# Fourier mixing beside attention on one core: the hidden-dimension transform by sums and differences of features n and n + 224

## The chip, the cores and the metric

The kernel runs on one core of a Trainium2 chip. The metric is the device time of one execution in microseconds (us); the time of a kernel is the median over its runs. Engines: TensorE (PE; PEld is its weight load), VectorE (DVE), ScalarE (ACT), GpSimd (POOL) and SyncE (SP), whose queue issues every DMA of this kernel.

## The reference

Two independent halves, written side by side. A is a two-dimensional Fourier transform of `x` (2048 tokens by 448 features), real part only, by given matrices; B is attention with 16 heads of 28 features over 2048 tokens.

```python
# S = 2048, D = 448; everything float32
a = einsum("bsd,ed->bse", A_x, dft_hid_re)
b = einsum("bsd,ed->bse", A_x, dft_hid_im)
A = einsum("ts,bse->bte", dft_seq_re, a) - einsum("ts,bse->bte", dft_seq_im, b)
q, k, v = (B_x @ wqkv) split into 3 x 16 heads of 28
B = concat_heads(softmax(q @ k.T * 28 ** -0.5) @ v) @ wo
out = concatenate([A, B], axis=-1)
```

## The kernel before

**Products in parts.** TensorE multiplies in a reduced float format. To keep float32 accuracy an operand is split: `hi` is its rounded copy (made by ScalarE) and `lo` the rest (made by VectorE), and a product is hi x hi + lo x hi + hi x lo. With 448 features in the contraction (three blocks of 128 rows and one of 64, whose hi and lo share a block) that makes 11 products where three full ones would be 12.

**Stages.** In TensorE's order: the projections of `B_x` (L572, `chain`), then A's hidden transform (`hidden_both`, also through `chain`, L572), then the sequence transform of A in two parts, real and imaginary (`sequence_halved`, L909), each with a small middle row (`middle`, L857), and the output projection of B (`project_late`, L1372, and its last feature block, L1403). All of these are "fill work" around the attention: scores (`score`, L1138: one 128 x 512 product each, 1024 of them), exponentials on ScalarE (L1142), and attention times values (`four`, L1149). The latter runs in 64 bursts of 16 products, one burst per 16 exponentials. A burst of a whole chunk is followed by a normalization (`normal`): ScalarE copies the sums out (L1202), and DMAs carry them through memory (`sm`, L1206; `rd`, L1211; spread over partitions, L1215), VectorE multiplies (L1218), and the result goes to memory (L1221). The last head is handled chunk by chunk: its four chunks are folded by TensorE first (L1229), and `project_late` loads the last 64 features of each chunk (L1390), splits them (L1392, L1393) and adds their products (L1403, 8 per chunk, two per token tile).

**The hidden transform.** For each of 16 token tiles the features of the tile arrive with one DMA (`Piece`, L542) in a `wraw` buffer. The wanted 896 columns (448 real, 448 imaginary) are symmetric: column 448 - n equals column n up to sign. So only `MAIN` = 225 columns of each half (450) are computed in full with 11 products; for the other `REST` = 223 (446) four products with a difference table `w_rest` (all but zero for true Fourier matrices) are computed. That is 15 products per tile. The tables are built by `weights_both`, which also records the largest magnitude of the difference tables in `diff`. At the end of the kernel a flag is computed from `diff`; if the matrices are not what the symmetry assumes, a slower general path runs after it. With the given inputs it does not.

**Combining.** `combine` loads the stored results of tiles g and g + 8 (L788), copies two of them (L792), and forms sums and differences (L794, L795) which it splits (L797 hi on ScalarE, L798 lo on VectorE) into operands of the sequence transform, in the large buffer `big`. There are 8 groups g for each of the two parts, and with 4 copies a group 32 copies a part on ScalarE. The sequence transform's own weights come in units of four DMAs (L891), of which three go to buffers (`wdraw`) that lie where the hidden tables were, so they wait for the last hidden product.

**Buffers.** `kept` has 19 buffers of 128 x 1024 floats; each holds two exponential tiles, or a stored result, or a load. There are eight PSUM banks: four for fill work and four for scores, which may borrow from the former.

**What sets the order.** A planner in the kernel (`Schedule`) emits all instructions of all engines in one list, before the program runs. Every task has a key (a due time), durations and latencies; at each modelled moment an engine takes the ready task with the lowest key for which buffers are free. Constants set the keys: `T_ATT` and `T_END` spread the heads' scores, `T_FILL` the fill work, `T_OUT` the end, and `PE_TURN` and the 0.2146 per product are modelled prices of a burst. A DMA task without `hold` may be issued as soon as SP is idle and a buffer is free. On the chip each engine runs its list in order and waits on semaphores.

Of the kernel before, what the change touches and what calls it, by code (L numbers as in the profile page):

```python
# [14 lines left out]
ALU = mybir.AluOpType  # L15
# [48 lines left out]
def f32(ap):  # L64
    return ap.bitcast(F32)
# [16 lines left out]
PE_TURN = 0.33  # L82
# [231 lines left out]
def tile_kernel(ctx, tc, xa, wre, wim, wd, xb, wqkv, wo, out):  # L314
# [75 lines left out]
    nc.gpsimd.memset(diff[:, 2 * NQ, 4:3 * QT], 0.0)  # L390
# [51 lines left out]
    T_ATT, T_END, T_FILL, T_OUT = 28.0, 723.0, 850.0, 801.0  # L442
# [19 lines left out]
    F_HIDDEN = NT * 15 * M448  # L462
# [259 lines left out]
    w_hi = wd_t[:, :8 * MAIN].rearrange("p (k c) -> p k c", k=4)  # L722
    w_rest = wd_t[:, 8 * MAIN:8 * D].rearrange("p (k c) -> p k c", k=4)
    w_lo = big[:, 7 * S:7 * S + 8 * MAIN].rearrange("p (k c) -> p k c", k=4)

    def weights_both(key, after):
        ready = []
        for k in range(4):
            pair = kept_s.slot()
            at = key + 0.6 * k  # L730
            n = P if k < 3 else 64
            main = lambda t, n=P: t[:n].rearrange("p (a b) -> p a b", a=2)
            ld = dma(at, lambda pair=pair, k=k: nc.sync.dma_start(pair.t[:, :, :D], wd[:, k].rearrange("p (a b) -> p a b", a=2)), 448, use=[pair])
            a = act(at, lambda pair=pair, k=k: nc.scalar.activation(main(w_hi[:, k]), pair.t[:, :, :MAIN], AF.Copy), 0.45,
                    deps=[ld, *after], use=[pair])
            ts = [dve(at, lambda pair=pair, k=k, n=n: nc.vector.tensor_tensor(
                main(w_lo[:, k], n), pair.t[:n, :, :MAIN], main(f32(w_hi)[:, k], n), op=ALU.subtract), 0.55, deps=[a], use=[pair])]
            for i, op in ((0, ALU.subtract), (1, ALU.add)):
                ts.append(dve(at, lambda pair=pair, k=k, i=i, op=op: nc.vector.tensor_tensor(
                    w_rest[:, k, i * REST:(i + 1) * REST], pair.t[:, i, MAIN:D], back(pair.t[:, i], 1, REST), op=op), 0.3,  # L740
                    deps=[ld, *after], use=[pair]))
            seen.append(dve(at + 5, lambda k=k: nc.vector.tensor_reduce(
                diff[:, 2 * NQ, k:k + 1], f32(w_rest)[:, k], axis=AX.X, op=ALU.max, apply_absolute_value=True), 0.55, deps=ts))
            if k == 0:
                seen.append(dve(at + 5, lambda: nc.vector.tensor_reduce(
                    whole[:, 2 * NQ:2 * NQ + 1], f32(w_hi)[:, 0], axis=AX.X, op=ALU.max, apply_absolute_value=True), 0.55, deps=[a]))
# [747 lines left out]
```

## Time and profile before

| | |
|---|---|
| time, median of 3 runs | 825.43 us (825.27 to 826.31) |
| the profiled execution's own time | 829.04 us |
| its span, first to last instruction | 827.2 us |
| mean granted TensorE clock | 0.991 |
| TensorE matmul instructions in the trace | 4856 |

An instruction of the kernel's text on TensorE can appear as more than one row: attention times values has 1024 products in the program and 2048 rows in the trace. In a row of the groups by line the columns are line, engine, operation, tiles, shapes and count, then busy time and mean duration of one in ns, then idle time of the engine before them and what ended it. In a row of a window they are the stretch, its length, and for PE, PEld, DVE, ACT and POOL the busy time and count, then granted clock, DMA share and GB/s. In the chain of waits a row is a start, a length and what ran; in the timeline also the shape. TensorE's durations overlap (matmuls are pipelined), so what one costs is read from the distance between starts.

### The profile page before, as it was taken

The numbers are of one execution on the slowest core, as the hardware profiler recorded it, in microseconds if no ns is written. First come the engines' busy times: TensorE is split into PE (matmuls) and PEld (weight loads), VectorE is DVE, ScalarE is ACT, GpSimd is POOL, SyncE is SP. The second block draws the span as 40 slices with busy tenths as digits, with TensorE's granted clock in tenths as the row PEclk, the third lists the DMA queues.
The fourth block names the chain that finished last, engine by engine and source line by source line (L and its number), as shares of the span: only waits on it lengthen the run. The fifth ranks groups of instructions, "written<-read, shape, count | busy, mean of one in ns | idle before, by whom it ended". The sixth has DMA issues, their size and how long they took to land.

```text
span 827.2 us, 14140 instructions
## 1 busy us (share of the span) xinstructions
PE 814.4 (98%) x4856; PEld 531.0 (64%) x4856; DVE 383.2 (46%) x882; ACT 622.9 (75%) x1277; POOL 8.3 (1%) x59
## 2 busy tenths in 40 slices
PE   8999999999999999999989999999999999999996
PEld 7886555655566666656655675666766656665686
DVE  7541103123112134222367774566887585575561
ACT  6116888889888777878888877778997777778931
POOL 3000000000000000000000000000000000000000
PEclk9999999999999999999988999999999999999998
DMA  9847635334344434433487755359877756652643
GB/s 307 280 139 239 192 107 169 97 105 141 103 150 122 131 123 135 136 134 122 143 195 228 244 160 175 117 169 275 210 227 232 213 165 200 198 188 83 198 152 128
DMA packets 131535, 141.27 MB, mean 171 GB/s; under 512 B 36414, under 2 KB 100416, under 8 KB 131456
## 3 DMA queue, kind: packets, MB, share of 16 engines
q1 hardware_dynamic: 131456, 140.29, 54.7%
q8 instruction: 40, 0.66, 0.3%
q14 instruction: 39, 0.32, 0.1%
HBM read 98.82 MB, written 43.12 MB: 172 GB/s over the span
## 4 chain that ended last, share of the span: by engine, by line
PE 88%; ACT 5%; DMA 4%; DVE 1%; issue 1%; SPq 0%; ACTq 0%; DVEq 0%
PE bank L1138 28%; PE bank L1149 25%; PE bank L572 19%; PE bank L909 9%; PE bank L1372 4%; ACT kept L1142 3%; DMA wdraw<-wre 2%; PE bank L857 1%; PE bank L1122 1%; DMA wraw<-wre 1%; ACT big L797 1%; PE bank L1403 1%; DMA kept<-xb 1%; ACT big L792 1%; PE bank L1229 0%
## 5 line engine op out<-in xcount | busy, mean ns | idle before, releaser
L1142 ACT ACTIVATE kept<-bank 128x512 f32<-128x512 f32 x1024 | 511.1, 677 | 118.8 <-PE bank L1138 118.4
L1138 PE MATMUL bank<-q,k 85*128 85x512 f32 x1024 | 371.0, 409 | 1.6 <-DVE kept L1125 0.9
L1138 PEld LDWEIGHTS bank<-q,k 85*128 85x128 f32 x1024 | 186.4, 189 | 98.3 <-issue 42.0
L1149 PE MATMUL bank<-kept,v 128*32 128x512 f32 x2048 | 237.6, 605 | 0.0
L1149 PEld LDWEIGHTS bank<-kept,v 128*32 128x32 f32 x2048 | 60.8, 111 | 134.9 <-issue 127.6
L909 PE MATMUL bank<-big,wlo 128*128 128x226 f32 x512 | 104.4, 277 | 1.0 <-DVE wlo L899 1.0
L909 PEld LDWEIGHTS bank<-big,wlo 128*128 128x128 f32 x512 | 95.7, 198 | 9.8 <-DVE wlo L899 1.3
L572 PE MATMUL bank<-big,whi 128*128 128x512 f32 (+1 forms) x260 | 96.6, 392 | 0.9 <-ACT big L511 0.7
L909 PE MATMUL bank<-big,whi 128*128 128x448 f32 (+1 forms) x256 | 74.8, 325 | 1.1 <-DVE big L798 1.1
L881 DVE TENSOR_REDUCE diff<-wlo 128x1 f32<-128x512 f32 x96 | 65.5, 683 | 2.5
L439 DVE COPY kept<-bank 128x450 f32<-128x450 f32 (+2 forms) x43 | 26.7, 620 | 81.7 <-PE bank L572 71.1
L572 PEld LDWEIGHTS bank<-big,whi 128*128 128x128 f32 x260 | 49.3, 191 | 9.7 <-ACT big L511 1.1
L909 PEld LDWEIGHTS bank<-big,whi 128*128 128x128 f32 x256 | 49.1, 198 | 6.3 <-DVE big L798 1.4
L572 PE MATMUL bank<-big,wlo 128*128 128x512 f32 x112 | 44.2, 396 | 0.0
L614 DVE TENSOR_TENSOR wd<-bank,wd 128x512 fp32r<-128x512 f32 x16 | 10.9, 690 | 69.8 <-ACT wd L613 69.8
L572 PE MATMUL bank<-wd,whi 128*128 128x450 f32 (+1 forms) x128 | 41.6, 368 | 0.0
L899 DVE TENSOR_TENSOR wlo<-wraw,whi 128x512 fp32r<-128x512 f32 x32 | 22.1, 690 | 38.5 <-PE bank L909 34.8
L572 PE MATMUL bank<-wd,big 128*128 128x448 f32 x176 | 37.6, 370 | 0.0
L572 PEld LDWEIGHTS bank<-wd,big 128*128 128x128 f32 x176 | 32.9, 188 | 3.9 <-issue 0.7
L1372 PE MATMUL bank<-big 128*128 128x448 f32 x144 | 31.6, 366 | 0.0
L1202 ACT ACTIVATE kept<-bank 128x512 f32<-128x512 f32 (+1 forms) x19 | 11.6, 610 | 25.6 <-PE bank L1149 25.5
L928 DVE TENSOR_TENSOR wlo<-wdraw,wraw 128x256 fp32r<-128x256 f32 x64 | 24.3, 420 | 14.0 <-PE bank L909 13.3
(116 smaller groups left out, 576.5 us busy)
## 6 DMA issues: line engine op xcount, KB each, us to landing
wdraw<-wre SPq DMA_DIRECT2D x48, 256.0 KB
wdraw<-wim SPq DMA_DIRECT2D x48, 256.0 KB
qkd<-wd SPq DMA_DIRECT2D x32, 256.0 KB
q<-qkd SPq DMA_DIRECT2D x64, 112.0 KB
k<-qkd SPq DMA_DIRECT2D x64, 112.0 KB
abd<-kept SPq DMA_DIRECT2D x16, 448.0 KB
kept<-abd SPq DMA_DIRECT2D x16, 448.0 KB
qkd<-kept SPq DMA_DIRECT2D x24, 256.0 KB
```

Of the source, the lines that this page charges most:

```text
L439: nc.vector.tensor_copy(dst, src)
L572: nc.tensor.matmul(o.t[:, :cols], w(), x(), start=(i == 0), stop=(i == n - 1))
L614: b = dve(key, lambda o=o, hi=hi, lo=lo: nc.vector.tensor_tensor(as_r(lo.t), o.t, as_f(hi.t), op=ALU.subtract), deps=[a], use=[o, *own])
L881: seen.append(dve(key, lambda: nc.vector.tensor_reduce(dst, f32(flat(src.t)), axis=AX.X, op=ALU.max, apply_absolute_value=True), 0.6, deps ...
L899: b = dve_on(key - 11.5, lambda e: e.tensor_tensor(turned(lo.t), read(same.t), f32(turned(hi.t)), op=ALU.subtract), 0.65, deps=[a], acq=[l ...
L909: nc.tensor.matmul(o.t[:, at0:at0 + n], cut_of(w.t, e, c), x(), start=first, stop=stop)
L928: e.tensor_tensor(turned(dl.t, c, 2, HP), read(r.t, c, 2, HP), read(base.t, c, 2, HP), op=op)
L1138: m = pe(key, lambda e: nc.tensor.matmul(b.t, KT[h][kt // 4].t[:KR + 1, kt % 4 * P:(kt % 4 + 1) * P], q.t[:KR + 1, :], start=True, stop=True),
L1142: return act(key - 20, lambda: nc.scalar.activation(p.t, b.t, AF.Exp, scale=SCALE), deps=[m], use=[b, pair])
L1149: nc.tensor.matmul(o.t[j * VW:(j + 1) * VW, :], VT[h].t[:, kt // 4, kt % 4, :], tiles[i // 2].t[:, i % 2, :], start=(kt < 4 // len(cs)), s ...
L1202: a = act(key - 20, lambda: nc.scalar.activation(osb.t[:n * VW], o.t[:n * VW], AF.Copy, accum_out=sums[:n * VW, g:g + 1]), deps=[dep], use ...
L1372: nc.tensor.matmul(o.t[:, :D], a(), b(), start=(i == 0), stop=(i == 8 and n < N_HELD))
```

## The change

Features n and n + 224 are added and subtracted. With X the input and W a column of the table, x0 w0 + x1 w1 = (x0 + x1)/2 (w0 + w1) + (x0 - x1)/2 (w0 - w1). For true Fourier matrices w0 + w1 is zero in odd columns and w0 - w1 in even ones. There are four contraction blocks: sums of 128 and of 96 features (i = 0, 1), differences of 128 and 96 (i = 2, 3). All four are multiplied in hi with all 450 main columns and all 446 rest columns. The low parts, of the rows and of the tables, are used only for half the main columns: the even ones (226) for sums, the odd ones (224) for differences. So a tile has four products of 450 columns, four of 446, and eight of 226 or 224.

The tables for this are built by `weights_both` (2 x 3 loads in place of 4). The rows are loaded for tiles g and g + 8 together (`rows_both`, five DMAs into one `kept` buffer without `hold`, in place of one DMA per tile into a `wraw` buffer), and summed, subtracted and split by `folded`. The main results leave PSUM in two strided evictions (even, odd) and the rest in one.

```diff
-PE_TURN = 0.33
+PE_TURN = 0.22
-    T_ATT, T_END, T_FILL, T_OUT = 28.0, 723.0, 850.0, 801.0
+    T_ATT, T_END, T_FILL, T_OUT = 24.0, 666.0, 867.0, 788.0
-    F_HIDDEN = NT * 15 * M448
+    F_ROWS = 8 * M448 + 8 * MLOW
+    F_HIDDEN = NT * F_ROWS
...
+    def rows_both(g, key):
+        x = kept_s.slot()
+        at = lambda p0, p1, q: x.t[p0:p1, :, q * P:(q + 1) * P]
+        src = lambda p0, p1, k: xa[g:g + HT + 1:HT, p0:p1, k].rearrange("a p s -> p a s")
+
+        def put():
+            nc.sync.dma_start(x.t[:, :, :2 * P], xa[g:g + HT + 1:HT, :, :2].rearrange("a p k s -> p a (k s)"))
+            for q in range(2):
+                nc.sync.dma_start(at(0, 32, 2 + q), src(96, P, 1 + q))
+                nc.sync.dma_start(at(32, P, 2 + q), src(0, 96, 2 + q))
+        return x, dma(key, put, 128, n=5, use=[x])
+
+    def folded(x, ld, a, key):
+        hi, lo, raw = whi.slot(), wlo.slot(), wraw.slot()
+        q = lambda i: x.t[:, a, 2 * i * P:2 * (i + 1) * P].rearrange("p (k s) -> p k s", k=2)
+        d = [dve(key, lambda i=i, op=op: nc.vector.tensor_tensor(raw.t[:, 2 * i:2 * i + 2], q(0), q(1), op=op), 0.37,
+                 deps=[ld], use=[x, raw]) for i, op in enumerate((ALU.add, ALU.subtract))]
+        h = act(key + 1, lambda: nc.scalar.activation(hi.t, raw.t, AF.Copy, scale=0.5), ACT_S, deps=d, acq=[hi], use=[raw])
+        l = dve(key + 1.5, lambda: nc.vector.scalar_tensor_tensor(
+            lo.t, raw.t, 0.5, f32(hi.t), op0=ALU.mult, op1=ALU.subtract), 0.68, deps=[h], acq=[lo], use=[raw, hi])
+        return hi, lo, h, l
+
     def hidden_both(ready):
...
-            both = products(hi, lo, x3, lambda k: (lambda: w_hi[:, k]), lambda k: (lambda: w_lo[:, k]))
-            rest = [(hi(k), (lambda k=k: w_rest[:, k])) for k in range(3)] + [(x3(), lambda: w_rest[:, 3])]
...
+        for g in range(HT):
+            x, ld = rows_both(g, fkey(0, 0) - 13)
...
+                for i in range(4):
+                    c0, c1 = (0, EVEN) if i < 2 else (EVEN, 2 * MAIN)
+                    seq += [(hi, i, lambda i=i: table(i, "main"), 0, 2 * MAIN, M448), (lo, i, lambda i=i: table(i, "hi"), c0, c1, MLOW),
+                            (hi, i, lambda i=i: low_at[i][:ROWS[i % 2]], c0, c1, MLOW)]
+                rest = [(hi, i, lambda i=i: table(i, "rest"), 0, 2 * REST, M448) for i in range(4)]
...
-        pv = pe(key, emit, d=0.2146 * NT, deps=[*es, *got_v[h]], use=[*tiles, VT[h], po], mode=1)
+        pv = pe(key, emit, d=0.2046 * NT, deps=[*es, *got_v[h]], use=[*tiles, VT[h], po], mode=1)
...
-    combine(0, lambda g: max(s_at - 18 + 4 * g, h_at + (s_at - h_at) * (g + 1) / HT), lambda g: x_users if g < HT - 1 else [h_last])
+    combine(0, lambda g: max(s_at - 50 + 6 * g, h_at + (s_at - h_at) * (g + 1) / HT), lambda g: x_users if g < HT - 1 else [h_last])
```

The constants and the shorter hidden transform give the planner another order. In the changed file lines stand further down: scores are L1196, bursts L1207, exponentials L1200, the hidden transform L816, the sequence transform L967, combining L850 and L855, output products L1430, their last part L1461, the fold L1287.

ScalarE, first copies of `combine` for part 0. Before (516 exponentials stand ahead of the first, 562 ahead of the last):

```order
L1142 ACTIVATE kept_239<-bank_271 128x512
L1142 ACTIVATE kept_239<-bank_270 128x512
L792 ACTIVATE big<-kept_235 128x226 x2
L797 ACTIVATE big<-kept_236 128x448 x2
L792 ACTIVATE big<-kept_253 128x226 x2
L797 ACTIVATE big<-kept_246 128x448
```

In the change (355 exponentials ahead of the first, 450 ahead of the last):

```order
L1200 ACTIVATE kept_237<-bank_276 128x512
L1200 ACTIVATE kept_239<-bank_275 128x512
L850 ACTIVATE big<-kept_240 128x226 x2
L855 ACTIVATE big<-kept_241 128x448 x2
L850 ACTIVATE big<-kept_235 128x226 x2
L855 ACTIVATE big<-kept_249 128x448
```

The groups of copies look alike; they begin while the hidden transform still runs (its last product stands at score 411 in the change, at 514 before) and are spread over twice as many exponentials.

TensorE, shortly after the last hidden product, in the change:

```order
L967 MATMUL bank_271<-big,wlo_214 128x226
L1196 MATMUL bank_277<-q_228,k_219 128x512
L967 MATMUL bank_272<-big,wlo_214 128x226
L1196 MATMUL bank_274<-q_225,k_219 128x512
L1196 MATMUL bank_275<-q_226,k_219 128x512
L1196 MATMUL bank_270<-q_227,k_219 128x512
L1196 MATMUL bank_277<-q_228,k_219 128x512
L1196 MATMUL bank_274<-q_225,k_219 128x512
L1196 MATMUL bank_275<-q_226,k_219 128x512
L1196 MATMUL bank_273<-q_227,k_219 128x512
L1196 MATMUL bank_277<-q_228,k_219 128x512
L1196 MATMUL bank_274<-q_225,k_220 128x512
```

Eleven scores follow one another with no sequence product between (two more stand after the last row shown). Before, the longest such row at this place had eight. A second row of eleven stands in the change some 95 scores before the last one.

TensorE at the end of the program, before:

```order
L1403 MATMUL bank_274<-big,q_227 128x448 x2
L1403 MATMUL bank_277<-big,q_227 128x448 x2
L1372 MATMUL bank_272<-big 128x448 x9
L1372 MATMUL bank_273<-big 128x448 x9
L1372 MATMUL bank_271<-big 128x448 x9
L1372 MATMUL bank_270<-big 128x448 x9
L1372 MATMUL bank_272<-big 128x448 x9
L1372 MATMUL bank_273<-big 128x448 x9
L1403 MATMUL bank_271<-big,q_228 128x448 x2
```

and in the change:

```order
L1461 MATMUL bank_274<-big,q_227 128x448 x2
L1461 MATMUL bank_276<-big,q_227 128x448 x2
L1430 MATMUL bank_273<-big 128x448 x3
L1430 MATMUL bank_270<-big 128x448 x9
L1430 MATMUL bank_272<-big 128x448 x9
L1461 MATMUL bank_271<-big,q_228 128x448 x2
```

Ahead of the last chunk's products (`q_228`) there are 21 output products in place of 54. Counted from the last fold, 76 output products and 18 products of the last part stand before them in the change, 118 and 24 before.

107 lines of the change are left out of this document (67 added, 40 removed).

## The prediction

> **What bounds the kernel now.** I read the page first: busy shares, then its chain of waits.
>
> ```profile
> span 827.2 us, 14140 instructions
> PE 814.4 (98%) x4856; PEld 531.0 (64%) x4856; DVE 383.2 (46%) x882; ACT 622.9 (75%) x1277; POOL 8.3 (1%) x59
> PE 88%; ACT 5%; DMA 4%; DVE 1%; issue 1%; SPq 0%; ACTq 0%; DVEq 0%
> ```
>
> TensorE holds 88% of the chain that ended last, so the kernel is the length of TensorE's instruction stream plus the few places where that stream waits. Second is ScalarE: its exponentials decide how fast scores can follow one another. The groups by line and shape price both.
>
> ```profile
> L1142 ACT ACTIVATE kept<-bank 128x512 f32<-128x512 f32 x1024 | 511.1, 677 | 118.8 <-PE bank L1138 118.4
> L572 PE MATMUL bank<-wd,whi 128*128 128x450 f32 x64 | 23.6, 369 | 0.0
> L572 PE MATMUL bank<-big,whi 128*128 128x450 f32 x64 | 23.7, 370 | 0.0
> L572 PE MATMUL bank<-wd,wlo 128*128 128x450 f32 x48 | 17.7, 369 | 0.0
> L572 PE MATMUL bank<-wd,whi 128*128 128x446 f32 x64 | 18.8, 368 | 0.0
> ```
>
> An exponential costs ScalarE 511.1/1024 = 0.50 us. The four L572 rows are the hidden transform: 64+64+48+64 = 240 products of 450 or 446 columns. Their durations (369 ns) overlap, so the step from one to the next is read from the chain of waits in a busy stretch:
>
> ```profile
> 301.17 3.57 PE bank L1149 x32
> 306.10 0.41 PE bank L572 x2
> 306.51 0.70 PE bank L1138 x3
> ```
>
> A wide product is 0.205 us, a score 0.233, a burst of attention-times-values 3.57. For half the width I take the products of the sequence transform, two of which stand between two scores in the timeline:
>
> ```profile
> 443.02 0.39 PE L909 MATMUL bank<-big,wlo 128*128 128x226 f32 x2
> 443.25 0.40 PE L1138 MATMUL bank<-q,k 85*128 85x512 f32 x1
> ```
>
> 443.25 - 443.02 = 0.23 for two, 0.115 each.
>
> Two places matter beside the stream itself. One is the change from the hidden to the sequence transform:
>
> ```profile
> 412.28:448.68 36.40, 33.95 (x178) 19.93 (x181) 23.62 (x61) 30.67 (x69) 0.00 (x0) 0.86 0.79 203
> L1138 PE MATMUL bank<-q,k 85*128 85x512 f32 x46 | 17.4, 424 | 0.4 <-ACT kept L1142 0.2
> L909 PE MATMUL bank<-big,wlo 128*128 128x226 f32 x39 | 8.1, 280 | 1.0 <-DVE wlo L899 1.0
> L909 PE MATMUL bank<-big,whi 128*128 128x448 f32 x12 | 4.5, 379 | 0.0
> L909 PE MATMUL bank<-big,whi 128*128 128x226 f32 x12 | 3.5, 293 | 1.1 <-DVE big L798 1.1
> ```
>
> In these 36.4 us (from the end of one burst to the start of another, two bursts between) TensorE did 46 scores (10.7 us), two bursts (7.1), 51 narrow products (5.9) and 12 wide ones (2.5): 26.2 us of work, so 10.2 us are lost. Why, the chain and the windows show:
>
> ```profile
> 414.56 4.69 ACT kept L1142 x9
> 420.10 5.41 DMA wdraw<-wre
> 433.21 0.40 DVE big L798
> 413.00:419.50 6.50, 6.13 (x27) 3.63 (x29) 4.17 (x13) 6.50 (x16) 0.00 (x0) 1.00 0.81 75
> 419.50:423.00 3.50, 3.50 (x20) 0.87 (x16) 1.70 (x6) 3.50 (x10) 0.00 (x0) 0.51 0.89 183
> 433.20:440.00 6.80, 6.35 (x29) 1.67 (x33) 5.02 (x14) 4.41 (x11) 0.00 (x0) 0.50 0.96 275
> ```
>
> Scores run at ScalarE's pace, then the first sequence weights and the last combined operand (L798) are late, and twice the granted clock falls to a half, for 3.5 and 6.8 us: some 5 of the 10.2 us.
>
> The other place is the end:
>
> ```profile
> 780.38 0.39 PE L1138 MATMUL bank<-q,k 85*128 85x512 f32 x1
> 788.39 0.97 PE bank L1229 x2
> 789.37 9.56 PE bank L1372 x46
> 807.77 10.88 PE bank L1372 x54
> 818.65 0.42 PE bank L1403 x2
> 792.70 0.52 SPq L1206 DMA_DIRECT2D sm<-kept  x1
> 797.28 0.35 SPq L1211 DMA_DIRECT2D rd<-sm  x1
> 799.64 0.54 SPq L1215 DMA_DIRECT2D kept<-rd  x1
> 804.40 0.67 DVE L1218 TENSOR_TENSOR kept<-kept 32x512 f32<-32x512 f32 x1
> 807.12 1.10 SPq L1390 DMA_DIRECT2D kept<-ond  x2
> 812.65 0.69 DVE L1393 TENSOR_TENSOR q<-kept,q 64x512 fp32r<-64x512 f32 x1
> 789.43 0.57 ACT L1202 ACTIVATE kept<-bank 32x512 f32<-32x512 f32 x1
> ```
>
> After the last chunk's fold (ends 789.36) its normalization goes through five DMAs and is ready at 813.34 (812.65 + 0.69): 24.0 us, of which about 2.7 (ScalarE's copy ends at 790.0, the DMA is issued at 792.7) is the first DMA held in SP's queue. TensorE needs it at 818.65. So the chain has 5.3 us to spare now, covered by output products (0.205 each). From the last score (780.38) to the end of the span are 46.8 us.
>
> **The change part by part.** *The hidden transform.* 240 wide products become 128 wide ones (eight a tile: four main, four rest) and 128 of 226 or 224 columns. Before: 240 x 0.205 = 49.2 us. After: 128 x 0.205 + 128 x 0.115 = 41.0 us. That is -8.2 us. Bounds: half width at half the price (0.103) gives -9.8; if a narrow product had to wait for a whole weight load, which the next row puts at 198 ns, it gives 26.2 + 25.3 = 51.5, +2.3. The measured 0.115 is itself a product with a weight of its own, so I take it.
>
> ```profile
> L909 PEld LDWEIGHTS bank<-big,wlo 128*128 128x128 f32 x512 | 95.7, 198 | 9.8 <-DVE wlo L899 1.3
> ```
>
> The Trainium skill (TensorE: Matmul & The Clock Gate, section LDWEIGHTS (loading the stationary operand)) prices a weight load by its columns at 1.2 GHz, 107 ns for 128; as an estimate from that page narrow products would be floored there, 128 x 0.107, and the term would be -9.3. By that rule the 198 ns of the row are not the floor, and the trace's 0.115 agrees.
>
> *What the transform needs.* VectorE gains 32 sums or differences of 256 columns, and the low part is made of 512 columns instead of 384 + 128; there is one more eviction a tile. SP issues 40 row loads in place of 16, and 6 table loads in place of 4, 26 issues at about 0.35 to 0.55 us (the SP rows above), so 9 to 14 us spread over about 200 us. VectorE's cover:
>
> ```profile
> 300.00:350.00 50.00, 50.00 (x302) 30.49 (x301) 16.44 (x34) 38.60 (x80) 0.00 (x0) 1.00 0.44 139
> ```
>
> It is busy a third of that time while TensorE is full; I cost all this at nothing. If the cover were gone, each late tile would hold the queue for about one VectorE instruction, 0.7 us (L1218's row), 11 us over 16 tiles.
>
> *The entrance to the sequence transform.* Combining moves ahead: in the order of the change its 32 groups of copies stand between exponentials 355 and 450, before between 516 and 562, so 64 copies meet 95 exponentials instead of 46. What stays: the weight loads L891 (420.10: 5.41 us) may only start after the last hidden product. The order pays for that with a row of scores and no other work: eleven of them, which ScalarE paces at 0.50 against 0.233, 11 x 0.267 = 2.9 us. I take the hole from 10.2 to 2.9 plus a third of the old clock loss, 1.8: -5.5 us. Bounds: -10.2 (all covered) and 0 (the same hole at the new place). The entrance of the second sequence transform has as dense a cluster as before, 32 copies in 60 exponentials both times: 0.
>
> *The end of attention.* The sequence transform now ends before attention does, and the output products that replace it need their operands from ScalarE first. Once more eleven scores stand alone, about 95 scores before the end: +2.9, against half as long a row of scores before: I take +1.5 (0 to 2.9).
>
> *The tail.* In the new order there are 76 output products and 18 last-part products between the last fold and the last chunk's products (118 and 24 before): 94 x 0.205 = 19.3 us of cover for a chain of 24.0. Without the 2.7 us in SP's queue the chain is 21.3, with as much again 26.7, so TensorE waits 2.0 to 7.4 us at the end; I take 4. The DMAs before it in SP's queue wait for VectorE's final additions, so some hold remains.
>
> *Sum*: -8.2 - 5.5 + 1.5 + 4 = **-8.2 us**. As a cross-check from the end: the last score has within 1 us the same TensorE work ahead of it in both orders. It comes 5.5 earlier by the entrance, 1.5 later by the lone scores, 0.9 later by work; the chain behind it gives 9.0 (score to fold's end) + 24.0 + 8.5 (818.65 to 827.2) = 41.5 instead of 46.8, -5.3: -8.4 together. The profiled span of 827.2 would be about 819. The median of the runs shown, 825.43, lies 1.8 under that span, so I forecast **817.2 us**.
>
> **The rivals.** (1) *The hole only moves.* The eleven lone scores last 11 x 0.50 = 5.5 us with TensorE half used; the 6.5 us before 419.5 looked like that and ended in a half clock. Against it: the operands are combined earlier. If the entrance loses its 10.2 again, 817.2 + 5.5 = 822.7; with a second dip at the other lone row (+2 to 3) 825, no measurable change.
>
> (2) *The holes close.* No dip, a tail with the 21.3 us chain, both lone rows half covered (1.5 left at the entrance, 0.5 at the end of attention): -8.2 - 8.7 + 0.5 + 2.0 = -14.4, so 811. For it: ahead of the end the two windows above hold the only dips, both in a stretch short of work.
>
> The Trainium skill (TensorE: Matmul & The Clock Gate, section The HAM clock gate (the "warmup" mystery)) says that the clock halves after an idle window of about 3.4 us. By it the lone scores, with TensorE half busy, would cause no dip, the 1.8 would go, and the sum would be 815.4, inside the forecast's range. The trace does not bear the rule out in this form: in the 6.5 us before 419.5 TensorE started 27 instructions and still lost its clock.
>
> (3) *Slower: buffers.* The row loads take kept buffers, carry no hold, and are issued as soon as SP is free: eight of the 19 are taken long before the hidden transform reads them. A round of 16 exponentials needs eight. The new order already shows the squeeze: three early rounds have their burst right at the round's end, and then 60 projection products run with one score among them. If exponentials wait for a buffer on the chip where the order expects none, the scores' banks stay full and TensorE's stream stands. The place is scores 96 to 360, 16 rounds. At 1 us a round it is +16, so 833. It decides from 8.2 / 16 = 0.5 us, one exponential, a round. Against it: fill work is there to run, and ScalarE is at 38.6 of 50 in that stretch.
>
> (4) *It does not do what it says*: narrow products at the weight load's 198 ns give +2.3 for the first term, 827.7. The 0.115 step nearly excludes it.
>
> **How the numbers follow.** A difference under about 0.2% (1.7 us) can't be told from none here. Forecast (814 to 821): 0.45. Rival 2 (808 to 814): 0.20. Rival 1 (821 to 827): 0.20, of which about 0.06 within 0.2%. Rival 3 (over 827): 0.12. Rival 4: 0.03, half of it within 0.2%. So faster 0.45 + 0.20 + 0.14 = 0.79, the same 0.07, slower 0.14. All terms low give -18.0 (807.4), all high +12.6 (838); the range 809 to 825 leaves out the lowest end and rival 3.
>
> **What would show it.** Right: the hidden transform's 256 products at 41 us of steps; no loss of 10 us between its last product and the fourth burst after it; the last four output groups waiting for L1393's counterpart, 2 to 7 us, with the end 41 to 42 us after the last score. Wrong: granted clock at 0.5 for 10 us or more in the middle, TensorE waiting for exponentials between scores 96 and 360, or narrow products at 0.2 us.

## The result and the profile after

| | before | the change |
|---|---|---|
| time, median (4 runs each, side by side) | 825.52 us (825.27 to 826.31) | 829.69 us (827.46 to 831.62) |
| ratio, 95% interval | | 1.0040 (1.0021 to 1.0059) |
| the profiled execution's own time | 829.04 us | 827.46 us |
| its span | 827.2 us | 825.6 us |
| mean granted clock, profiled execution | 0.991 | 0.993 |

The change makes the kernel slower by 0.4%, 4.2 us. The two profiled executions say the opposite, -1.6 us. The one of before was 3.5 us slower than its median and the one of the change 2.2 us faster than its own; -1.6 + 3.5 + 2.2 gives the 4.2.

From the page of the changed kernel come the span, the busy shares and the chain of waits by engine; from its groups by line and shape the exponentials and the hidden transform's widest groups.

```profile
span 825.6 us, 14220 instructions
...
PE 807.9 (98%) x4872; PEld 524.5 (64%) x4872; DVE 399.6 (48%) x925; ACT 619.2 (75%) x1274; POOL 7.9 (1%) x58
...
PE 93%; DMA 2%; ACT 2%; SPq 1%; DVE 0%; issue 0%; ACTq 0%
...
L1200 ACT ACTIVATE kept<-bank 128x512 f32<-128x512 f32 x1024 | 510.7, 673 | 107.0 <-PE bank L1196 106.2
...
L816 PE MATMUL bank<-wd,whi 96*128 96x450 f32 x32 | 11.9, 372 | 0.0
L816 PE MATMUL bank<-wd,whi 128*128 128x450 f32 x32 | 11.8, 370 | 0.0
L816 PE MATMUL bank<-wd,whi 128*128 128x446 f32 x32 | 11.8, 369 | 0.0
L816 PE MATMUL bank<-wd,whi 96*128 96x446 f32 x32 | 11.8, 368 | 0.0
```

The wide products are the 128 that were announced, and they last what they lasted. The narrow ones show in the timeline of TensorE, by the distance between starts:

```profile
301.60 0.27 PE L816 MATMUL bank<-wd,wlo 128*128 128x226 f32 x1
301.70 0.28 PE L816 MATMUL bank<-big,whi 128*128 128x226 f32 x1
301.82 0.37 PE L816 MATMUL bank<-wd,whi 96*128 96x450 f32 x1
302.02 0.27 PE L816 MATMUL bank<-wd,wlo 96*128 96x226 f32 x1
```

They step by 0.10 to 0.12 us. Summed from start to start over all its products, the hidden transform takes 41.6 us of TensorE instead of 50.7: 9.0 us less, where 8.2 were forecast. The work is gone, and yet the time rose. Where it went is seen when the span is cut at certain scores (counted from 0, by the start of each in the trace). The hidden transform runs between scores 258 and 514 before, between 178 and 411 in the change. The last five columns belong to the experiments below.

| stretch, us | before | change | short products, order of before | change, rows held, constants of before | before, column loads moved | held, column loads moved | the same, replanned |
|---|---|---|---|---|---|---|---|
| start to score 0 | 55.0 | 50.5 | 55.6 | 55.6 | 55.9 | 55.6 | 55.5 |
| 0 to 192 | 137.9 | **160.0** | 137.9 | 138.1 | 138.1 | 138.1 | 138.1 |
| 192 to 512 (hidden transform) | 213.7 | 213.9 | 212.7 | 211.0 | 213.6 | 211.4 | 211.1 |
| 512 to the last | 373.8 | 359.8 | 371.8 | 373.0 | 367.0 | 363.8 | 361.2 |
| last score to the end | 46.8 | 41.4 | 46.7 | 46.8 | 47.1 | 47.8 | 47.1 |
| span | 827.2 | 825.6 | 824.6 | 824.6 | 821.8 | 816.8 | 813.0 |

The change starts its attention 4.5 us earlier, is 22.1 us longer up to score 192, as long as before from there to score 512, and 19.4 us shorter behind it. A longer stretch need not be a lost one, since work can have moved into it. So TensorE's work is taken out: each step, from start to start, counts at the median of its kind in that profile, a burst at 3.57 us. What a stretch lasts beyond that work is lost time.

| us beyond TensorE's work | before | change | change, constants of before, rows not held | the same, rows held | short products | held, column loads moved |
|---|---|---|---|---|---|---|
| start to score 192 | 5.7 | 7.3 | 11.3 | 6.0 | 6.2 | 6.0 |
| 192 to 512 | 4.1 | 8.9 | 17.4 | 7.3 | 12.3 | 7.7 |
| 512 to 576 | 10.4 | 1.4 | 1.5 | 8.5 | 9.2 | 1.9 |
| 576 to the last | 13.7 | 19.3 | 27.7 | 16.8 | 13.0 | 14.8 |
| last score to the end | 7.6 | 11.8 | 12.9 | 7.8 | 7.6 | 8.6 |
| TensorE's work | 785.5 | 776.9 | 779.0 | 778.2 | 776.2 | 777.7 |

In the change the work is 8.6 us less. Another 9 us are won between scores 512 and 576, where before has its entrance to the sequence transform. Almost all of it is lost elsewhere: 1.6 us up to score 192, 4.8 from there to score 512 (some 3.5 of them at the change's own entrance, at 350 to 375 us), 5.6 between score 576 and the last, 4.2 behind the last. Of the 22.1 us up to score 192 almost all, 21.2, are work that was done earlier: TensorE has 156.8 us of work there instead of 135.6.

That work moves forward mostly at scores 80 to 160. First ScalarE's timeline in the changed kernel, then TensorE's groups in the stretch 140 to 166 us:

```profile
145.99 6.96 ACT L1200 ACTIVATE kept<-bank 128x512 f32<-128x512 f32 x14
152.67 0.77 ACT L614 ACTIVATE wd<-bank 128x512 fp32r<-128x512 f32 x1
...
164.49 0.59 ACT L614 ACTIVATE kept<-bank 128x512 fp32r<-128x512 f32 x1
165.41 1.09 ACT L1200 ACTIVATE kept<-bank 128x512 f32<-128x512 f32 x2 [0.33 <-ACT kept L614]
```

```profile
L573 PE MATMUL bank<-big,whi 128*128 128x512 f32 x50 | 17.0, 398 | 0.0
L573 PE MATMUL bank<-big,wlo 128*128 128x512 f32 x29 | 11.5, 395 | 0.0
L1196 PE MATMUL bank<-q,k 85*128 85x512 f32 x17 | 5.9, 397 | 0.0
```

For 12.5 us (152.9 to 165.4) ScalarE takes no exponential. TensorE is never idle: in the 26 us of the second view it runs 79 products of the projection, 17 scores and a burst. An exponential writes to a `kept` buffer, and by then the row loads have taken theirs. The first is issued at 19 us and the last group at 145 us, in SyncE's timeline; the last of these buffers is read at 309 us. With rows held (an experiment below) the first is issued at 228 us. First two rows of the change, then one of the held kernel:

```profile
19.42 0.80 SPq L780 DMA_DIRECT2D kept<-xa  x1
...
144.87 0.39 SPq L780 DMA_DIRECT2D kept<-xa  x1
```

```profile
227.85 0.41 SPq L780 DMA_DIRECT2D kept<-xa  x1
```

TensorE waits for nothing in this stretch. What it spends here is fill work. That this work is then missing beside later scores is argued from the table, where the time is lost late.

The end behaves as forecast (4.2 us more beyond the work, where 4 were taken). In the chain of waits the last chunk's operand arrives late, and TensorE stands:

```profile
806.90 0.42 PE bank L1461 x2
...
810.02 0.45 SPq L1448
...
810.52 3.46 DMA kept<-ond
...
814.72 0.70 DVE q L1451
...
815.46 0.69 PE bank L1461 x2
```

```profile
815.46 0.88 PE L1461 MATMUL bank<-big,q 128*128 128x448 f32 x3 [2.67 <-DVE q L1451]
```

The second fence is TensorE's timeline: 2.67 us idle ahead of the last products.

### The profile page after: what moved, and what is told of

It reads as the page before. It is cut to its first block, busy times and chain, and to the rows that moved or that the text cites. A ratio compares the mean times of both kernels' runs of the same rounds, so it can differ in the third digit from the quotient of the medians.

```text
span 825.6 us, 14220 instructions
## 1 busy us (share of the span) xinstructions
PE 807.9 (98%) x4872; PEld 524.5 (64%) x4872; DVE 399.6 (48%) x925; ACT 619.2 (75%) x1274; POOL 7.9 (1%) x58
## 4 chain that ended last, share of the span: by engine, by line
PE 93%; DMA 2%; ACT 2%; SPq 1%; DVE 0%; issue 0%; ACTq 0%
PE bank L1196 31%; PE bank L1207 27%; PE bank L573 13%; PE bank L967 12%; PE bank L816 5%; PE bank L1430 3%; ACT kept L1200 1%; PE bank L915 1%; PE bank L1180 1%; DMA kept<-xb 1%; DMA wraw<-wim 1%; DMA kept<-abd 1%; PE bank L1461 1%; PE bank L1287 0%; DMA kept<-ond 0%
## 5 line engine op out<-in xcount | busy, mean ns | idle before, releaser
L1200 ACT ACTIVATE kept<-bank 128x512 f32<-128x512 f32 x1024 | 510.7, 673 | 107.0 <-PE bank L1196 106.2
L1196 PE MATMUL bank<-q,k 85*128 85x512 f32 x1024 | 374.4, 413 | 3.6 <-ACT kept L1200 3.6
L1196 PEld LDWEIGHTS bank<-q,k 85*128 85x128 f32 x1024 | 186.5, 189 | 100.5 <-issue 39.0
L1207 PE MATMUL bank<-kept,v 128*32 128x512 f32 x2048 | 233.9, 597 | 0.0
L1207 PEld LDWEIGHTS bank<-kept,v 128*32 128x32 f32 x2048 | 60.6, 110 | 130.8 <-issue 124.3
L967 PE MATMUL bank<-big,wlo 128*128 128x226 f32 x512 | 106.6, 277 | 0.0
L967 PEld LDWEIGHTS bank<-big,wlo 128*128 128x128 f32 x512 | 96.3, 198 | 9.5 <-issue 0.7
L967 PE MATMUL bank<-big,whi 128*128 128x448 f32 (+1 forms) x256 | 74.6, 323 | 0.0
L573 PE MATMUL bank<-big,whi 128*128 128x512 f32 x196 | 69.6, 398 | 2.3 <-ACT big L512 1.4
L967 PEld LDWEIGHTS bank<-big,whi 128*128 128x128 f32 x256 | 49.6, 198 | 5.0 <-ACT kept L1200 0.5
L439 DVE COPY kept<-bank 128x226 f32<-128x226 f32 (+4 forms) x63 | 30.3, 502 | 42.5 <-PE bank L816 39.0
L573 PEld LDWEIGHTS bank<-big,whi 128*128 128x128 f32 x196 | 36.8, 189 | 12.5 <-ACT big L512 1.8
L816 PE MATMUL bank<-wd,whi 128*128 128x450 f32 (+3 forms) x128 | 42.7, 369 | 0.0
L1430 PE MATMUL bank<-big 128*128 128x448 f32 x144 | 37.1, 366 | 0.0
```

The lines of the kernel that those rows point to most:

```text
L439: nc.vector.tensor_copy(dst, src)
L573: nc.tensor.matmul(o.t[:, :cols], w(), x(), start=(i == 0), stop=(i == n - 1))
L816: nc.tensor.matmul(o.t[:, c0:c1], of(w, i), y(), start=n == 0, stop=n == m)
L967: nc.tensor.matmul(o.t[:, at0:at0 + n], cut_of(w.t, e, c), x(), start=first, stop=stop)
L1196: m = pe(key, lambda e: nc.tensor.matmul(b.t, KT[h][kt // 4].t[:KR + 1, kt % 4 * P:(kt % 4 + 1) * P], q.t[:KR + 1, :], start=True, stop=True),
L1200: return act(key - 20, lambda: nc.scalar.activation(p.t, b.t, AF.Exp, scale=SCALE), deps=[m], use=[b, pair])
```

## The experiments

The first four ask what the change's parts do alone: the hold of the row loads, and the new constants with the earlier combination. The eleven ran in three sittings (the first four, the next four, the last three), each with runs of before beside it: medians 828.05, 827.43 and 829.06 us. Across sittings the ratios are compared. The stretches come from one profiled execution of each kernel.

**Hold alone.**

```diff
-        return x, dma(key, put, 128, n=5, use=[x])
+        return x, dma(key, put, 128, n=5, hold=True, use=[x])
```

> The changed kernel with one word more: the row loads (five DMAs per pair of tiles) carry hold, so they take a kept buffer only shortly before the hidden transform reads them. Buffer theory (the early row loads take eight of 19 kept buffers, scores fall 14 to 21 us behind between scores 96 and 160, fill work is used up early and is missing behind the last score): the score of number 160 comes within 3 us of the old kernel's 171.7 us, TensorE no longer waits at the end, time 819 to 825. Constants theory (the new planner constants make rows of lone scores and clock dips, the buffers don't matter): the order still has rows of 15 and 16 lone scores, so 828 or more. Cost theory (the new transform itself costs as much as it saves): no better than 829.

Measured 848.56 us, ratio 1.0269 (1.0216 to 1.0323), as the constants theory had it. Score 160 starts at 175.3 us instead of 192.7 (3.6 us behind before's), so the squeeze is gone, and the last score at 771.9 instead of 784.2. But the order that the planner then makes has rows of 8, 15, 15 and 16 scores with hardly anything between them from score 781 on, and leaves all output products for after the last score. The 12 us won at the last score are more than lost behind it: 74.9 us from there to the end, where the change has 41.4, with a half-clock window of 10.2 us at 788.

**New constants alone**, on the kernel before: `T_ATT` to `T_OUT`, `PE_TURN`, the 0.2046 of the burst, and the combination from -50 in steps of 6.

> The old kernel with only the constants of the change (T_ATT to T_OUT, PE_TURN, 0.2046, the combine keys). Buffer theory: no row loads here, so within 2 us of the old kernel's 825.5. Constants theory: slower, 829 or more, with lone scores around scores 530, 770 and 1000.

Measured 845.64 us, ratio 1.0232 (1.0198 to 1.0266): by themselves they cost 18 us. The buffer theory, by which nothing should have changed here, can't be the whole account.

**Old constants, no hold**: the change with these four set back.

> The change with the old constants, row loads still without hold. Buffer theory: score 160 again 15 us or more behind, the last score no earlier than 784 us, the end uncovered, 828 to 835. Constants theory: the transform's 8 us appear, 817 to 821.

Measured 852.83 us, ratio 1.0294 (1.0234 to 1.0354), 18 us above the range of the buffer theory. Score 160 is 27.1 us behind before's, the last score at 806.9 us.

**Old constants and hold.**

> The change with hold on the row loads and with the old constants. Buffer theory and constants theory together: 8 to 9 us under the old kernel, 815 to 819, the last score near 771 us, 28 us or more of output products behind the last fold. Cost theory: 824 or more, with waits of TensorE on VectorE or DMAs inside the hidden transform.

Measured 824.84 us, ratio 0.9979 (0.9955 to 1.0003), not told apart from before. That is the number of the cost theory, but not its mechanism: inside the hidden transform TensorE waits for 0.7 us in all. Score 160 is 0.6 us behind before's. The last two kernels differ in the one word `hold` and by 28.0 us: row loads that take buffers early are a loss of that size under these constants. In the two profiles the time beyond TensorE's work falls from 70.8 to 46.4 us, and only 5.3 of that ahead of score 192: the rest is lost later. The change's own constants go with the squeeze: with the hold they give 848.56 us, and the squeeze without them gives 852.83, each some 20 us worse than the two together. But the 9.0 us of TensorE don't come out here either: 3 us, if anything.

**Short products alone.** Is a shorter transform worth its TensorE time? The same order as before, instruction for instruction:

```diff
+                m = MAIN + 1 if i in few else cols
+                nc.tensor.matmul(o.t[:, :m], w(), x()[:, :m] if i in few else x(), start=(i == 0), stop=(i == n - 1))
-                nc.tensor.matmul(o.t[:, :cols], w(), x(), start=(i == 0), stop=(i == n - 1))
```

> The kernel before with its own order of instructions on every engine, in which six of the eleven low and main products of each hidden tile (96 in all) write 226 of their 450 columns. The low parts of the other 224 columns are left out. This is the first term of the sum alone: 96 x (0.205 - 0.11) = 9.1 us of TensorE work less, with nothing moved. If the length of TensorE's stream sets the time where the hidden transform runs, the time falls by 7 to 9 us (before 828 on this chip: 819 to 821) and the first score after the transform comes as much earlier. Rival: the shorter transform only makes TensorE wait longer at the entrance to the sequence transform, whose loads and combined operands come when they did; then 3 us or less are gained (825 or more).

Measured 826.11 us, ratio 0.9983 (0.9966 to 1.0001). The rival's number holds: about 1 of 9 us is gained, if anything. But not for its reason. The gain is missing long before the entrance: from score 256 to 512 the kernel takes 169.7 us and before 170.7. ScalarE's timelines show why, first before, then short products:

```profile
294.71 7.94 ACT L1142 ACTIVATE kept<-bank 128x512 f32<-128x512 f32 x16 [1.91 <-PE bank L1138]
305.45 7.46 ACT L1142 ACTIVATE kept<-bank 128x512 f32<-128x512 f32 x15 [2.79 <-PE bank L1138]
```

```profile
294.77 7.95 ACT L1143 ACTIVATE kept<-bank 128x512 f32<-128x512 f32 x16 [1.87 <-PE bank L1139]
305.44 7.46 ACT L1143 ACTIVATE kept<-bank 128x512 f32<-128x512 f32 x15 [2.73 <-PE bank L1139]
```

In each round of 16 scores ScalarE runs its exponentials without a gap, waits some 2 us while TensorE is in its burst (the bracket), and starts again 10.7 us later, in both kernels. TensorE's rows are full before, and ScalarE's round is just as long. The saved time can be found again: over these rounds the steps of the 256 scores sum to 68.0 us with short products, to 62.7 before.

**Short exponentials**, to test that: with the short products, and as a control with before's. All engines keep the order of before.

```diff
-        return act(key - 20, lambda: nc.scalar.activation(p.t, b.t, AF.Exp, scale=SCALE), deps=[m], use=[b, pair])
+        return act(key - 20, lambda: nc.scalar.activation(p.t[:, :448], b.t[:, :448], AF.Exp, scale=SCALE), deps=[m], use=[b, pair])
```

> The narrow-product kernel (order of before, 9.1 us of TensorE work less) in which each exponential takes 448 of its 512 columns; the other 64 columns of each score tile are left out, and the score tiles are set to zero at the start. In the narrow-product run the 16 rounds from score 256 to score 512 lasted 169.7 us, as before (170.7), though TensorE had some 8 us less to do there. Theory: ScalarE's 16 exponentials of 0.50 us and what stands between them last as long as TensorE's work in each of these rounds, so less TensorE work alone gains nothing; with some 0.05 us less an exponential (0.8 us a round) the gain comes out, and those 16 rounds last 160 to 163 us. Rival: the fixed order itself, or loads, hold those rounds; then they stay at 169 to 170.

> The kernel before with the same shortened exponentials (448 of 512 columns, 64 left out, score tiles set to zero at the start). It is the control: TensorE keeps its 9.1 us there. Theory of two equal limits: the rounds from score 256 to score 512 stay within 2 us of before's 170.7, since TensorE's own work fills them. Rival, ScalarE alone sets those rounds: they fall by as much as in the narrow-product kernel with short exponentials.

ScalarE's timelines again, short products first, the control second:

```profile
292.49 7.09 ACT L1145 ACTIVATE kept<-bank 128x448 f32<-128x448 f32 x16 [2.28 <-PE bank L1141]
302.66 6.66 ACT L1145 ACTIVATE kept<-bank 128x448 f32<-128x448 f32 x15 [3.08 <-PE bank L1141]
```

```profile
295.27 7.09 ACT L1144 ACTIVATE kept<-bank 128x448 f32<-128x448 f32 x16 [2.81 <-PE bank L1140]
305.94 6.66 ACT L1144 ACTIVATE kept<-bank 128x448 f32<-128x448 f32 x15 [3.57 <-PE bank L1140]
```

| score 256 to 512, us | full exponentials | 448 columns |
|---|---|---|
| products of before | 170.7 | 169.6 |
| short products | 169.7 | 161.6 |

Either relief alone is worth 1 us, both together 9. In these rounds of before's order TensorE and ScalarE are equally long, and what is taken from one is spent waiting for the other. The times, 823.96 us with before's products and 815.61 with short ones (ratios 0.9932 and 0.9844, three and two runs), also hold what shorter exponentials do elsewhere, so the stretch is what is compared.

**The entrances.** What made the holes there? In the kernel before, SyncE's queue at the first entrance reads:

```profile
409.67 1.94 SPq L891 DMA_DIRECT2D wdraw<-wre  x3
411.65 0.65 SPq L834 DMA_DIRECT2D edge<-wre  x1
412.34 5.76 SPq L831 DMA_DIRECT2D edge<-wre  x3
...
419.64 0.41 SPq L788 DMA_DIRECT2D kept<-abd  x1
420.10 2.99 SPq L891 DMA_DIRECT2D wdraw<-wre  x3
```

Four loads of single columns of the transform (`columns`) stand in a row. The first (L834) takes 0.65 us, the three behind it hold the queue for 5.76 us, 1.9 us each where other loads take some 0.4 to 0.65. Shortly behind them stand the operand and the weights for which TensorE then waited. These loads were given to GpSimd's queue, which leaves TensorE, ScalarE and VectorE as they were:

```diff
-        edge_ready[part] = [dma(key + i, lambda i=i: nc.sync.dma_start(
+        edge_ready[part] = [dma(key + i, lambda i=i: nc.gpsimd.dma_start(
-        ld = dma(key, lambda: nc.sync.dma_start(raw, src[HT, :, :, 0]), 64, extra=4.0, deps=after)
+        ld = dma(key, lambda: nc.gpsimd.dma_start(raw, src[HT, :, :, 0]), 64, extra=4.0, deps=after)
```

> The kernel before, in which GpSimd's queue issues the eight loads of single columns of the transform (four at each entrance to a sequence transform) instead of SyncE's; TensorE, ScalarE and VectorE keep every instruction in its place. In the profile of before three of them hold SyncE's queue for 5.76 us (412.34 to 418.1) right ahead of the sequence weights (420.10) and of a combined operand (419.64) that TensorE then waits for, and for 4.77 us (588.92) at the second entrance. Theory: the holes at the entrances are made by SyncE's queue, not by the copies of the combination on ScalarE and VectorE. Then those loads start about 6 and 5 us earlier and the time falls by 4 to 8 us (820 to 824 where before is 828). Rival, as the prediction had it: the dense copies of the combination make the hole; then the time stays within 1 us of before.

Measured 823.96 us, ratio 0.9965 (0.9950 to 0.9980), 3.5 us less, a little under the 4 to 8 of the theory. In its profile GpSimd issues the first set at 102 us and SyncE has the operand's load out at 415.29 instead of 419.64:

```profile
103.24 3.43 POOL L831 DMA_DIRECT2D edge<-wre  x3
```

```profile
415.29 0.41 SPq L788 DMA_DIRECT2D kept<-abd  x1
415.75 1.48 SPq L891 DMA_DIRECT2D wdraw<-wre  x3
417.33 0.41 SPq L788 DMA_DIRECT2D kept<-abd  x1
```

From score 512 to 576 it takes 46.3 us where before's profiled execution took 52.7, and the granted clock stays whole until after the last score. The half clock of that one execution of before is part of the difference, so the medians, 3.5 us apart, are the better measure.

> The changed kernel with the same move of the eight column loads to GpSimd's queue. In its profile they hold SyncE's queue for 4.59 us from 357.22 and for 4.34 us from 534.84; behind them the operand load of 368.29 and the weights of 551.59 come late, and TensorE loses 4.0 and 4.9 us there. Theory of the queue: most of these 8.9 us return, so 5 to 8 us less than the changed kernel's 829.7 (822 to 825). Rival, copies of the combination: no change. Second rival: the late wait at the end (2.8 us) grows by as much as the entrances win, since the end's chain has no cover: 1 to 3 us less.

Measured 830.07 us, ratio 1.0040 (1.0026 to 1.0054) against before, the very ratio of the change itself: nothing gained. Here the theory of the queue fails. The chain of waits of this kernel at its first entrance:

```profile
352.63 0.93 ACT big L855 x2
353.56 0.46 ACT whi L956
...
354.29 6.62 ACT kept L1200 x13
360.90 0.56 ACT big L850 x2
...
363.60 4.50 DMA wdraw<-wre
```

In the change's order ScalarE's own copies (L850, L855) and thirteen exponentials in a row lead the path, with a load behind them. TensorE still loses 3.0 us there (4.0 in the change); the second entrance wins 1 us too. In the two profiles that is lost again in the early stretch and at the end of attention. The end waits as before (2.68 us against 2.67), so the second rival, by which it would have waited longer, doesn't explain it.

> The changed transform with held row loads and the constants of before (824.8 in an earlier run), with the eight column loads on GpSimd's queue. In that kernel's profile they hold SyncE's queue for 6.09 us from 399.95, the operand load behind them lands at 414.0, and TensorE loses 8.3 us there and 5.3 us at the second entrance. Theory of the queue: 5 to 9 us less, 816 to 820. Rival, copies of the combination: no change (825). If the clock halves at the entrances for another reason than the hole, half of the gain is left: 821 to 823.

Measured 818.12 us (817.50 to 818.67), ratio 0.9889 (0.9868 to 0.9910): where the same kernel with the loads on SyncE had 0.9979 in another sitting, 0.9 points or some 7 us more. At the first entrance TensorE now loses 1.8 us instead of 8.3, at the second 3.6 instead of 5.3 (the excess of each step over the median of its kind, in the slices 400 to 425 and 575 to 600), and there is no half clock ahead of the end. Against before with its column loads moved, 823.96 in the same sitting, the changed transform is worth 5.8 us. By the first table it wins 2.2 us from score 192 to 512 and 3.2 behind that.

**Replanned.** What is left at the second entrance is again a cluster on ScalarE (in the chain of waits eleven exponentials from 583.00 to 588.22, then copies until 591). So the second combination was spread, and the planner was told the burst's length more exactly: `0.219`, `PE_TURN` 0.28, `T_ATT` 30, `T_OUT` 806, the second combination from -70 in steps of 6.

> The changed transform with held row loads and column loads on GpSimd's queue (818.1 in an earlier run), planned with the burst at the length that the profiles show (0.219 instead of 0.2146 for each step, its turn 0.28 instead of 0.33), T_ATT 30 and T_OUT 806, and the second combination spread over a longer stretch (from 70 instead of 40 ahead of its transform, 6 instead of 4 between groups). In the run that it changes TensorE still lost some 3.6 us between 575 and 600. Theory: what is left at the second entrance is the order's, so 1 to 4 us less, 814 to 817. Rival: it is paid for elsewhere, in lone rows of scores: 818 or more.

Measured 816.11 us (814.79 to 819.10), ratio 0.9862 (0.9840 to 0.9884). It is faster than before and than the change, inside the range of the theory, and the slice 575 to 600 loses 1.6 us instead of 3.6. Whether it is faster than the kernel ahead of it can't be said: the two intervals overlap.

## Why the prediction was wrong

The forecast was 817.2 us and faster; measured were 829.69 and slower. Three steps failed. The loss at the end of attention was sized at +1.5 and was about +4.5. What the early row loads do to the order was put at nothing. And the base was one execution that lay above its median. Of the 12.5 us between forecast and result, 6.6 lie between the span that was forecast, 819, and the span of the profiled change, 825.6; the rest lies between these two executions and their medians. Step by step:

*The hidden transform, -8.2.* As TensorE work the term was right (-9.0 by the steps). "The kernel is the length of TensorE's instruction stream" is another matter. Its own window (300 to 350 us) showed ScalarE at 38.6 of 50 and was read as room. But ScalarE can't use the rest: some 2 us of every round pass while the burst runs and no new score is to be had. The 2 by 2 table above shows two equal limits, and in before's order the term alone is worth 1.3 us, if anything (short products against before). In the change itself the planner laid the work out anew, and there the term did come out of the stretch: between 200 and 350 us TensorE loses 0.4 to 0.7 us in each 25 us, before 0.3 to 0.6 where its transform runs. A round lasts 10.5 us instead of 10.7, but the transform is through after 14.6 rounds instead of 16. With rows held and column loads moved it is worth 5.8 us of the 8.2.

*VectorE and SyncE, 0.* VectorE's extra 16 us hide, as said: no wait of TensorE shows in the hidden transform of the change. The row loads do not, though not by their time in the queue.

*Buffers.* This was rival 3, with a chance of 0.12. It named the buffers, the place (scores 96 to 360) and the 60 projection products with one score among them, and was set aside because "fill work is there to run". Its wait never came: TensorE stands for 0.0 us between scores 96 and 360. None of the prediction's three signs of being wrong appeared. The fill did run, 21.2 us of it too early, and the sign to look for was an idle ScalarE. What that costs is seen in the held and unheld kernels under before's constants, 28.0 us apart. In the change itself, planned with constants that go with it, the early row loads and these constants together cost about 0.6%, 5 us (ratios 1.0040 and 0.9979).

*The entrance, -5.5.* In the two profiles the stretch improves by about that: the excess at before's place (400 to 450, bursts included) falls from 10.2 to 1.5 us, and 350 to 375 rises from 0.4 to 4.0, -5.1 together. The size came out by luck, for two things in it were wrong. The cause of the hole in before was SyncE's queue behind the column loads, not the crowd of copies, though in the change's order the crowd does lead. (Of that crowd the prediction counted 64 copies among 95 exponentials; the first part has 32.) And the base was a bad one: in the thirteen runs of before of the first sitting the mean clock was 0.993 to 0.998, where the profiled one had 0.991 with two half-clock windows. The execution lay 3.6 us above its median. A time is some 1.8 us longer than its span (829.04 and 827.2), so a span of 819 is a time of 820.8; the working took 1.8 us off instead. How much of the -5.5 was in the median to be won isn't shown: with the column loads moved, 3.5 us were. The second entrance was put at 0 and loses 4.9 us (525 to 575), where before loses 3.6 (575 to 625).

*The end of attention, +1.5.* It was nearer 4.5: the slices 675 to 700 and 725 to 750 lose 2.9 and 3.9 us (0.7 and 1.6 in before), and the second holds a half-clock window. This is the largest miss among the terms of the sum.

*The tail, +4.* Right: a wait of 2.7 us, in the range of 2.0 to 7.4, and 41.4 us from the last score to the end, where the cross-check said 41.5. What that check had wrong was its first line, that the last score has the same work ahead of it and so comes 3 us earlier: it came 3.8 us later.

Rival 1 (the hole only moves) has the dip at the second lone row right, at 731.3 us, and the entrance wrong: it loses 4.0 us at the new place, not 10.2. Rival 2 (the holes close) needed an order without a dip. Rival 4 is refuted by the steps of 0.10 to 0.12 us. The kernel with rows held and column loads moved ends near the ratio that was forecast (0.9889; 817.2 to 825.43 is 0.990), but by another way, so that doesn't bear the prediction out.

Open: why the new constants cost before 18 us was followed only as far as the rows of lone scores and the clock. That the change's late losses at 695 to 735 us come from its early fill is argued from the pair with and without hold and was not tried by itself. And no single part, taken back alone, makes the change faster: the hold and the old constants pay only together.

## What to carry to other kernels

Before a saving on the busiest engine is counted as time, take one period of the loop and ask how long the second engine needs for the same period with the gaps that it can't fill; if that is as long, only the two together pay, or an order laid out anew. A load that may start early is not free because its queue is: count what its buffer would have been used for meanwhile. Fill work that runs in place of scores shows as no wait; take the work out of each stretch before calling it won or lost. When a hole is to be explained, read what stands ahead of the late transfer in its queue, and check with a second execution that the hole is there in the median.

## What the runs showed of the hardware

*Slow issues.* A load of one column (128 partitions of 16 single elements) delays the issue that stands behind it in SyncE's queue. Where such a load is the first of its row or stands apart, it takes 0.55 to 0.81 us, like other loads. In the change with constants of before and rows not held the four of the second entrance stand apart, and it is the ordinary loads behind them that are long (0.4 us is usual for L846):

```profile
541.66 0.39 SPq L846 DMA_DIRECT2D kept<-abd  x1
542.09 0.64 SPq L892 DMA_DIRECT2D edge<-wim  x1
542.77 2.48 SPq L846 DMA_DIRECT2D kept<-abd  x1
545.29 0.61 SPq L889 DMA_DIRECT2D edge<-wim  x1
546.00 2.33 SPq L1269 DMA_DIRECT2D rd<-sm  x1
```

Right behind another column load it took 1.3 to 3.2 us (in the kernel with old constants and hold). On GpSimd's queue each took 1.15 to 1.28 us. The Trainium skill (DMA: Bandwidth & Descriptors, section Issuing engine by pattern) puts simple loads on SyncE and calls that path generally faster. For a column load by itself the rows agree, for a row of them not: the four of before took 6.4 us of SyncE's queue and 4.7 of GpSimd's. Moving them was worth 3.5 and some 7 us in two orders and nothing in the third. Spreading them out on SyncE's queue was not tried.

*The clock.* Ahead of the last score, in all thirteen profiles, it fell to a half only after a stretch short of work: in the 3.4 us before each dip TensorE had at most 2.2 us of work (what starts there, each at the median step of its kind). Mostly scores ran at ScalarE's pace there; in others a load was late. These dips last 3.4 or 6.8 us. Two windows of the changed kernel, columns as before:

```profile
727.00:731.30 4.30, 3.57 (x12) 1.61 (x11) 0.00 (x0) 4.30 (x10) 0.00 (x0) 1.00 0.88 244
731.30:734.80 3.50, 3.50 (x15) 1.30 (x19) 0.00 (x0) 3.50 (x8) 0.00 (x0) 0.51 0.46 155
```

Twelve instructions start in the 4.3 us ahead of it, and TensorE counts as 83% busy. The Trainium skill (TensorE: Matmul & The Clock Gate, section The HAM clock gate (the "warmup" mystery)) lets the clock halve after an idle window of about 3.4 us; the length of the dip agrees, but TensorE did not have to be idle for a whole window. Not every such stretch costs the clock, and it differs from run to run. The change and the change with its column loads moved have the same order on TensorE: near 698 us both have 1.7 us of work in 3.4, and only the second has a dip there. The change's four timed runs have mean clocks of 0.986 to 0.993, and the six runs of the held kernel with its column loads moved 0.997 to 0.999. That the dip is caused by the lone scores was not isolated.
